# Set numbers of spare matmuls before the first batch's waits, and new due times throughout

## The chip, the core and the metric

The kernel runs on one core of a Trainium2 chip. The metric is device time in microseconds for one launch: the median of three runs before the change is 1341.77 us (1341.25 to 1344.07). Lower is better. TensorE is called PE in profiles, its weight loads PEld, VectorE is DVE, ScalarE is ACT, GpSimd is POOL, and SP is the engine whose queue issues nearly all DMA transfers.

## The reference

Attention over 32 learned memory slots (8 batches, 8 heads, 576 tokens, 64 wide), then two feed-forward layers over the 4608 tokens (512 to 2048 to 512, twice). Cut to what is computed:

```
a = softmax(phi over tokens);  k_m = a.T @ k;  v_m = a.T @ v
attn = softmax(q @ k_m.T / 8) @ v_m            # per batch and head
h = x @ w_in;   r = max(h, 0);  x = (s * r * r + b) @ w_out
h = x @ w1;     out = (h * sigmoid(1.702 * h)) @ w2
```

The weights are float64 in HBM and are turned into float32 on the chip.

## The kernel before, in words

The program is a list of operations, each with a due time, the engines that could run it with a cost on each, and the tiles it reads and writes. `Order.sort` (lines 90 to 184) is a list scheduler: it keeps a clock for each engine and always takes the ready operation that can start first, with rank (due time less a correction in the table `EARLIER`) deciding between several. What it writes out is one fixed order of instructions on each engine. Its clocks are only its own reckoning; on the chip each engine goes through its instructions in that order and waits at semaphores.

There are three large stages: eight batches of attention with the first matrix product; the product with `w_out` (the function `down`); and the second layer (`up`, then `last`). All large products run as three float32r matmuls (high and low halves of each operand), and the two large stages use a seven-product scheme for blocks, so that most of the DVE's and ACT's time goes to additions and to splitting operands.

The change is strongest in the opening of the first batch, where PE has no large product to do yet. Its chain on PE, by the names of the PSUM tiles:

- `warm`: ten matmuls of the identity with itself, of no use to the result.
- `s` (`slots`, line 586): two transposes of the maxima `am`; two that spread the negated maxima `nm`; 32 small products of `ph` (the exponentials) with `kv`, in two groups of 16, one per half of the heads (`mm`, line 631); eight more for the last 64 tokens (`last`, line 637); two transposes of the scaled result `an`. ACT then copies the slot keys `km`.
- `x` (`beside`, line 692): scores of `q` with `km`, in two pieces of 384 and 192 columns; each is copied to `sc` and folded back by transposes into `a` (line 727).
- `vw` (`matrix`, line 826): the slot values times the converted `w_in` block; ACT rounds it to `mh`, and PE subtracts `mh` from `vw` in place (line 850), which ACT copies to `ml`.
- `y` (line 740): transposes of the weights `st` after the softmax, from which ACT and DVE make `ah` and `al`.
- `h` (`step`, line 856): the first large product. From here on PE has dense work to the end.

When an operation on PE opens a PSUM tile, `pst` (line 274) may put spare matmuls ahead of it: each multiplies the 128 x 128 float32 identity by itself into the tile that is about to be overwritten. `Order.sort` sets their number just before the operation (line 163): the gap that the scheduler's own clock has there, in us, times `FILL` = 2.5. Tiles `x` and `a` of the first batch get none (line 276), and the second group of 16 and the last eight of `s` get none, since they open no tile. Spare matmuls go on until tile `warm` is opened a second time at the third block of the first batch (line 1484).

Of the kernel before, what the change touches and what calls it, by code (L numbers as in the profile page):

```python
# [18 lines left out]
P = 128  # L19
# [8 lines left out]
class Order:  # L28
# [4 lines left out]

    FILL, AHEAD, SLACK = 2.5, 120, 0.3

    EARLIER = {
        ('t', ('u4', 'wo', 5), 0): 16,
        ('t', ('e', 'w1', 0, 2)): -5,  # L40
        ('w', ('wi', 1, 0), 1): -3,
        ('w', ('mh', 0, 0)): -15,
        ('t', ('st', 0, 0)): -3,
        ('t', ('ol', 'wo', 2, 1, 1)): 5,
        ('t', ('al', 0, 0), 1): 1,
        ('t', ('ol', 'wo', 5, 1, 'A')): 14,
        ('sm', ('a', 1, 0, (0, 1))): 1,
        ('t', ('ah', 1, 0), 0): -3,
        ('w', ('w1', 7, 0, 1), 'l'): -12,
        ('sm', ('a2', 0, 1)): 21,  # L50
        ('t', ('sw1', 0, 0)): -12,
        ('t', ('A', 'wo', 0, 1)): -2,
        ('w', ('raw', ('w', ('wi', 1, 1)), 1), 0): 2,
        ('w', ('raw', ('w', ('wi', 1, 0)), 0), 0): -2,
        ('t', ('C', 'wo', 5, 3)): 5,
    }

    NEAR = 4
# [5 lines left out]
    def __init__(self, bufs):  # L64
        self.bufs, self.ops, self.rank, self.fill, self.until, self.since = bufs, [], [], None, 0, 0
        self.narrow = set()
        self.slot = {}
        self.wrote, self.read, self.users = {}, {}, {}

    def add(self, due, ways, r=(), w=(), first=0):  # L70

        n = len(self.ops)
        deps, new = set(), []
        for k in r:
            deps |= self.wrote[k]
            self.read.setdefault(k, set()).add(n)
        for k in w:
            deps |= self.wrote.get(k, set()) | self.read.get(k, set())
            self.wrote[k], self.read[k] = {n}, set()
        for x in dict.fromkeys(k[:2] for k in (*r, *w) if k[0] in self.bufs):  # L80
            if x not in self.users:
                self.users[x] = []
                new.append(x)
            self.users[x].append(n)
        deps.discard(n)
        due = max([due] + [self.ops[d][0] for d in deps])
        self.ops.append((due, ways, deps, new))
        self.rank.append(due - first - self.EARLIER.get(w[0] if w else None, 0))

    def sort(self):  # L90
# [22 lines left out]
        while ready:  # L113
            can = {}
            limit = ready[0][0] + self.AHEAD
            for due, n in ready:
                if due > limit and can:
                    break
                _, ways, deps, new = ops[n]
                t0 = 0.0  # L120
                if new:
                    ok = True
                    for tag in {x[0] for x in new}:
                        mine = [x for x in new if x[0] == tag]
                        f = free[tag]
                        if len(f) < len(mine) or any(x not in queue[tag][:len(f)] for x in mine):
                            ok = False
                            break
                        t0 = max(t0, f[0][0] if len(mine) == 1 else heapq.nsmallest(len(mine), f)[-1][0])
                    if not ok:  # L130
                        continue
                best = None
                for i, (eng, cost, _, port) in enumerate(ways):
                    t = max(t0, at.get(eng, 0.0))
                    if port:
                        t = max(t, held["dve" if eng == "pool" else "pool"])
                    for d in deps:
                        e = end[d] + (self.LAG[eng] if on[d] != eng else 0.05)
                        if e > t:
                            t = e  # L140
                    score = t + cost * self.WEIGHT.get(eng, 1.0)
                    if best is None or score < best[0]:
                        best = score, t, eng, i
                can.setdefault(best[2], []).append((best[1], due, n, best[3]))
            if not can:
                raise RuntimeError("no order")
            first = []
            for tag, v in can.items():
                t0 = min(v)[0]
                like = [c for c in v if c[0] <= t0 + 0.1 and c[2] in self.narrow and c[1] >= self.since] if tag == "pe" and run else ()  # L150
                if like:
                    c = min(like, key=lambda c: c[1:])
                    if c[1] < min(v, key=lambda c: c[1:])[1] + self.NEAR:
                        first.append(c)
                        continue
                first.append(min((c for c in v if c[0] <= t0 + (self.SLACK if c[1] < self.until else 0.0)), key=lambda c: c[1:]))
            t, _, n, i = min(first)
            _, ways, _, new = ops[n]
            eng, cost, fn, port = ways[i]
            if port:  # L160
                held[eng] = t + cost
            if self.fill and eng == "pe":
                out.append(lambda n=int((t - at.get(eng, 0.0)) * self.FILL): self.fill and self.fill(n))
            for x in new:
                queue[x[0]].remove(x)
                self.slot[x] = heapq.heappop(free[x[0]])[1]
            at[eng], on[n] = t + cost, eng
            end[n] = t + cost + self.END_LAG.get(eng, 0.0)
            ready.remove((rank[n], n))
            if eng == "pe":  # L170
                run = n in self.narrow
            out.append(fn)
            for m in after[n]:
                left[m] -= 1
                if not left[m]:
                    bisect.insort(ready, (rank[m], m))
            for x in of[n]:
                last[x] = max(last[x], end[n])
                uses[x] -= 1
                if not uses[x]:  # L180
                    heapq.heappush(free[x[0]], (last[x] + 0.2, self.slot[x]))
# [5 lines left out]
class Net:  # L187
# [27 lines left out]
    COL = 0.463  # L215

    FIRST = 100
    HEAD1 = (-51.0, 2.9, 16.5)
    PARTS1 = (-0.8, -1.7, -3.5)
    SCORES1 = (-34.0, 6.0, 7.5)  # L220
    COUPLES1 = (7.8, -36, 6.5)
    LEADS1 = (20, 17, 11, 10.0, 3, 1.6, 11.0, 1.3)
    VALUES1 = (-31.0, -1.6, 7.6, 28.4)
    VALUES = (-6.5, -9.4, 0.0, -1.9)
    NEXT1, NEXT = (6.0, 6.5), (-0.4, 1.9)
    ROWS1, ROWS = (24.5, 1.7, 0.3), (11, 10.5, 2.0)
    POOL1 = ((0, 1), (0,), (0,), (0,))
    TURN1 = (1, 1, 1, 1)
    EITHER1 = 0
    WAIT = 0  # L230
    OUT1 = (-12.1, 11.5)

    B1, B2 = 40, 58.5

    TS, N = 384, 6
    PAS, AT = 2.0892857142857144, 5
    PREP = (30, 100, 148.5, 222)

    def __init__(self, nc, tc, ctx, aps):
        self.nc, self.tc, self.a = nc, tc, aps  # L240
# [32 lines left out]

    def pst(self, k):
        x = self.t(k, [P, 2, 512])
        for _ in range(min(self.spare, 0) if k[1][0] in ('x', 'a') and k[1][1] == 0 else self.spare):
            self.nc.tensor.matmul(x[:, 0, 0:P], self.ident, self.ident, start=True, stop=True)
        self.spare = 0
        return x

    def dram(self, name, *index, cols=768):

# [303 lines left out]
    def slots(self, b, due, apart, lead=8):  # L586
# [25 lines left out]
        d = ds[1]  # L612
# [3 lines left out]
        for g in range(2):  # L616
# [13 lines left out]

            def mm(g=g, ph=ph, fs=fs):
                out = T[z] if g else self.pst(z)
                for c in range(4):
                    for h in range(4):
                        nc.tensor.matmul(out[32 * h:32 * h + 32, g, 0:129], T[ph][:, h, :, c], T[fs[h]][:, c], start=(c == 0), stop=False)
# [4 lines left out]
                        r = slice(64 * g, 64 * g + 64)  # L640
                        nc.tensor.matmul(T[z][32 * h:32 * h + 32, g, 0:129], T[phs[g]][r, h, :, 4], T[f1][r, h], start=False, stop=True)

            self.pe(d + 4, 2070, mm, (ph, *fs), (z,), narrow=True)
        self.pe(d + 4.5, 880, last, (*phs, f1), (z,), narrow=True)
        an = [("t", ("an", b, g)) for g in range(2)]

# [268 lines left out]
        us = range(t // self.HS, -(-(t + self.TS) // self.HS))  # L915
        self.dma(due, lambda: self.two(k).rearrange("p a b -> p (a b)"), lambda: self.rows(i, j, t, self.TS), [("r", i, j, u) for u in us], (k,), 384)

    FIRST2 = {1: -2.75, 6: -1.5, 7: 0.0, 5: 1.75, 3: 6.75, 'Y': 6.25, 4: 4.0}
    ODD2 = {1: -3.5, 6: 0.5, 7: 1, 5: 2, 'A': 4, 'B': 5, 3: 4, 4: 5.5, 'D': 6.5}
    EVEN2 = {1: -3.25, 6: 0, 7: 1, 5: 2, 3: 4, 'Y': 5, 4: 5.5}  # L920
    END2 = {1: -4, 6: 0, 7: 1, 5: 2, 'A': 3.25, 'B': 5, 3: 3, 4: 5, 'D': 5}
    ADDS = (0, 1, 2, 3, 4)
    LONG2 = {'Y': 1, 'A': 0.75, 'B': 0.75, 'D': 0.5}
    W1 = (30, 105, 2)
    LEAD2, EARLY2, AHEAD2, OD2, CC2 = 15, 9, 15.5, 1, 9

    def down(self, s, due):

# [330 lines left out]
            for k, t in ((old, s - 1), (new, s)):  # L1259
                self.out(due + 2, t, q, k)  # L1260

    HEAD = {1: -2.5, 6: 0, 7: 1, 5: 2, 'Y2': 2.5, 3: 3.5, 4: 5.5}
    MID = {1: -3, 6: -0.25, 7: 1.25, 5: 2.25, 'Y': 4.25, 'A': 4.75, 4: 5.25, 'B': 6.25, 'D': 7.25}
    END = {1: -3, 6: 0, 7: 1.25, 5: 2.25, 'A2': 3.25, 3: 3.75, 'B2': 4.75, 4: 5.75, 'D2': 5.75}
    AHEAD, OD, CC, RAW = 6, 3.0, 4.5, 2
    LONG = {'Y': 0.25, 'A': 0.75, 'B': 0.25, 'D': 0.25}
    EARLY, LEAD, BEGIN, T4 = 10.5, 8, -7.0, -6.8

    def last(self, s, due):

# [370 lines left out]
```

## Time and profile before

| | |
|---|---|
| median of three runs | 1341.77 us |
| the profiled execution | 1343.54 us, its span 1341.8 us |
| PE busy | 1326.7 us (99%) |
| DVE busy | 1147.3 us (86%) |
| ACT busy | 877.1 us (65%) |
| mean granted TensorE clock | 0.996 of 2.4 GHz |
| DMA moved | 381.29 MB, 284 GB/s |

PE is busy nearly all the time, so the interesting figure is its idle time, 15 us in all, and where it lies. A row of the time line that says `x20` holds 20 merged instructions; the number behind the start is the time from the first one's start to the last one's end, and in square brackets stands the idle time before the row and what ended it. Since matmuls overlap, the distance between the starts of two rows says what a row cost PE.

### The profile page before, as it was taken

How to read it: one execution, taken by the hardware profiler on the slowest of the kernel's cores; microseconds unless marked ns; L12 is line 12 of the kernel's file. 1: busy time of each engine (PE TensorE's matmuls, PEld its weight loads, DVE VectorE, ACT ScalarE, POOL GpSimd, SP SyncE). 2: the span in 40 equal slices, each digit the busy share in tenths (PEclk: the TensorE clock that was granted, in tenths of full speed). 3: DMA queues.
4: the chain of work that ended last, by engine and by line, in shares of the span. 5: the costliest groups of instructions: out<-in, count | busy, mean ns of one | idle time of the engine just before them, and what ended most of it. 6: DMA issues, size and time to landing. Idle time of an engine off the chain costs nothing.

```text
span 1341.8 us, 24315 instructions
## 1 busy us (share of the span) xinstructions
PE 1326.7 (99%) x9042; PEld 1284.1 (96%) x9042; DVE 1147.3 (86%) x1712; ACT 877.1 (65%) x1233; POOL 117.2 (9%) x112
## 2 busy tenths in 40 slices
PE   7999999999999999999999999999999999999998
PEld 5888888899999999999999999999999999999998
DVE  6887898999999999999997989696477698988985
ACT  4766666697877787889775666565464365655644
POOL 2201231100001000100100000000000011101011
PEclk8999999999999999999999999999999999999999
DMA  9988999896877695798799699879599978878984
GB/s 367 356 303 313 349 330 358 290 370 218 304 261 185 176 347 153 225 340 295 205 353 354 251 371 358 329 264 348 191 372 386 310 217 250 205 231 234 296 210 92
DMA packets 155959, 381.29 MB, mean 284 GB/s; under 512 B 17344, under 2 KB 30528, under 8 KB 155840
## 3 DMA queue, kind: packets, MB, share of 16 engines
q1 hardware_dynamic: 146048, 362.23, 75.7%
q0 software_dynamic: 9792, 17.50, 8.8%
q8 instruction: 71, 1.16, 0.3%
q14 instruction: 48, 0.39, 0.1%
HBM read 226.12 MB, written 153.55 MB: 283 GB/s over the span
## 4 chain that ended last, share of the span: by engine, by line
PE 94%; DVE 2%; DMA 2%; ACT 1%; issue 0%; SPq 0%; POOL 0%; POOLq 0%; ACTq 0%; DVEq 0%
PE h L344 5%; PE X L974 5%; PE X L975 5%; PE X L1182 5%; PE X L976 5%; PE X L1181 5%; PE X L1180 5%; PE h L346 5%; PE h L345 5%; PE X L1318 4%; PE X L1317 4%; PE X L1316 4%; PE Y L1182 2%; PE Y L1181 2%; PE Y L1180 2%; PE Y L975 2%
## 5 line engine op out<-in xcount | busy, mean ns | idle before, releaser
L344 PE MATMUL h<-ah,mh 128*128 128x288 f32 x512 | 156.0, 305 | 0.0
L320 DVE TENSOR_TENSOR ol<-A,oh 128x768 fp32r<-128x768 f32 x144 | 136.1, 954 | 22.5 <-ACT oh L314 12.6
L346 PE MATMUL h<-ah,ml 128*128 128x288 f32 x512 | 151.0, 295 | 0.1
L345 PE MATMUL h<-al,mh 128*128 128x288 f32 x512 | 150.7, 294 | 0.0
L314 ACT CAST oh<-A 128x768 fp32r<-128x768 f32 x125 | 107.3, 868 | 39.4 <-DVE A L320 18.9
L872 ACT ACTIVATE r<-h 128x576 f32<-128x576 f32 x127 | 89.5, 706 | 64.1 <-PE h L346 57.5
L974 PE MATMUL X<-oh,wo 128*128 128x384 f32 x384 | 128.5, 335 | 0.0
L975 PE MATMUL X<-ol,wo 128*128 128x384 f32 x384 | 128.4, 334 | 0.0
L976 PE MATMUL X<-oh,wo 128*128 128x384 f32 x384 | 128.3, 334 | 0.0
L1180 PE MATMUL X<-oh,w 128*128 128x384 f32 x384 | 128.3, 334 | 0.0
L1181 PE MATMUL X<-ol,w 128*128 128x384 f32 x384 | 128.3, 334 | 0.0
L1182 PE MATMUL X<-oh,w 128*128 128x384 f32 x384 | 128.3, 334 | 0.0
L344 PEld LDWEIGHTS h<-ah,mh 128*128 128x128 f32 x512 | 96.3, 188 | 17.4 <-issue 9.6
L1316 PE MATMUL X<-oh,w 128*128 128x384 f32 x320 | 107.0, 334 | 0.0
L1318 PE MATMUL X<-oh,w 128*128 128x384 f32 x320 | 106.9, 334 | 0.0
L346 PEld LDWEIGHTS h<-ah,ml 128*128 128x128 f32 x512 | 96.1, 188 | 0.3 <-ACT ml L853 0.3
L320 DVE TENSOR_TENSOR ol<-B,oh 128x768 fp32r<-128x768 f32 x96 | 89.8, 953 | 7.5 <-PE X L1318 3.6
L1317 PE MATMUL X<-ol,w 128*128 128x384 f32 x288 | 96.2, 334 | 0.0
L345 PEld LDWEIGHTS h<-al,mh 128*128 128x128 f32 x512 | 96.2, 188 | 0.0
L314 ACT CAST oh<-B 128x768 fp32r<-128x768 f32 x89 | 76.3, 870 | 25.9 <-DVE B L320 13.2
L974 PEld LDWEIGHTS X<-oh,wo 128*128 128x128 f32 x384 | 72.1, 188 | 0.4 <-ACT u L1000 0.4
L975 PEld LDWEIGHTS X<-ol,wo 128*128 128x128 f32 x384 | 72.1, 188 | 0.2 <-DVE ol L320 0.2
(323 smaller groups left out, 3818.0 us busy)
## 6 DMA issues: line engine op xcount, KB each, us to landing
w<-w SPq DMA_DIRECT2D x84, 512.0 KB, 5.9
r<-r SPq DMA_DIRECT2D x128, 288.0 KB, 4.7
kv<-in_kv SPq DMA_DIRECT2D x72, 258.0 KB, 5.4
g<-u SPq DMA_DIRECT2D x48, 384.0 KB, 4.2
raw<-in_w SPq DMA_DIRECT2D x32, 512.0 KB, 5.8
q<-in_q SPq DMA_DIRECT2D x32, 288.0 KB, 5.6
A<-r SPq DMA_DIRECT2D x24, 384.0 KB, 5.5
B<-r SPq DMA_DIRECT2D x24, 384.0 KB, 5.7
```

Source lines behind the costliest of these rows:

```text
L314: self.order.add(due, [self.act(n, lambda: nc.scalar.copy(out(), src()), psum), self.dve(n, lambda: nc.vector.tensor_copy(out(), src()), f ...
L320: self.order.add(due, [self.dve(n, lambda: nc.vector.tensor_tensor(out(), a(), b(), op=op), port=port)], r, w, first)
L344: self.nc.tensor.matmul(ps, wh, xh, start=start and i == 0, stop=False)
L345: self.nc.tensor.matmul(ps, wh, xl, start=False, stop=False)
L346: self.nc.tensor.matmul(ps, wl, xh, start=False, stop=(i == n - 1))
L974: nc.tensor.matmul(out, T[w][:, 0, c], T[h][:, p], start=f, stop=False, skip_group_check=True)
L975: nc.tensor.matmul(out, T[w][:, 0, c], T[l][:, p], start=False, stop=False, skip_group_check=True)
L976: nc.tensor.matmul(out, T[w][:, 1, c], T[h][:, p], start=False, stop=last, skip_group_check=True)
L1180: nc.tensor.matmul(out, T[w][:, 0, c], T[h][:, k], start=f, stop=False, skip_group_check=True)
L1181: nc.tensor.matmul(out, T[w][:, 0, c], T[l][:, k], start=False, stop=False, skip_group_check=True)
L1182: nc.tensor.matmul(out, T[w][:, 1, c], T[h][:, k], start=False, stop=k == 1, skip_group_check=True)
L1316: nc.tensor.matmul(out, T[w][:, 0, c], T[h][:, p], start=f, stop=False, skip_group_check=True)
```

## The change

The number of spare matmuls no longer follows from the scheduler's gaps but from a table, `SPARE`, keyed by the tiles that the operation writes. The second group of `s` and the scores `x` may have them too. Nearly all tables of due times have new values, and `EARLIER` has 27 entries in place of 17.

```diff
+    SPARE = {
+        (('ps', ('s', 0, 0)),): 12,
+        (('ps', ('s', 0, 2)),): 15,
+        (('ps', ('s', 0, 2)), ('ps', ('s', 0, 2), 1)): 29,
+        (('ps', ('s', 0, 3)),): 10,
+        (('ps', ('x', 0, 0)),): 13,
+        (('ps', ('vw', 0, 0)),): 8,
+        (('ps', ('y', 0, 0)),): 26,
+        (('ps', ('h', 0, 0, 0)),): 19,
+        (('ps', ('y', 0, 1)),): 4,
+        (('ps', ('h', 0, 0, 1)),): 7,
+        (('ps', ('s', 1, 0)),): 5,
+    }
...
-        ('t', ('e', 'w1', 0, 2)): -5,
+        ('t', ('e', 'w1', 0, 2)): -6,
...
+        self.opens.append(tuple(w))
...
-                out.append(lambda n=int((t - at.get(eng, 0.0)) * self.FILL): self.fill and self.fill(n))
+                out.append(lambda n=self.SPARE.get(self.opens[n], 0): self.fill and self.fill(n))
...
-    HEAD1 = (-51.0, 2.9, 16.5)
+    HEAD1 = (-53.0, 0.4, 32.0)
...
-    EITHER1 = 0
+    EITHER1 = 1
...
     def pst(self, k):
         x = self.t(k, [P, 2, 512])
-        for _ in range(min(self.spare, 0) if k[1][0] in ('x', 'a') and k[1][1] == 0 else self.spare):
-            self.nc.tensor.matmul(x[:, 0, 0:P], self.ident, self.ident, start=True, stop=True)
+        self.idle(x, 0)
+        return x
+
+    def idle(self, x, g):
+        for _ in range(self.spare):
+            self.nc.tensor.matmul(x[:, g, 0:P], self.ident, self.ident, start=True, stop=True)
         self.spare = 0
-        return x
...
             def mm(g=g, ph=ph, fs=fs):
                 out = T[z] if g else self.pst(z)
+                if g:
+                    self.idle(out, 1)
...
-            self.pe(d + 4, 2070, mm, (ph, *fs), (z,), narrow=True)
+            self.pe(d + 4, 2070, mm, (ph, *fs), (z, (*z, 1)) if g else (z,), narrow=True)
...
-    ODD2 = {1: -3.5, 6: 0.5, 7: 1, 5: 2, 'A': 4, 'B': 5, 3: 4, 4: 5.5, 'D': 6.5}
+    ODD2 = {1: -3.5, 6: 0.5, 7: 1, 5: 1.5, 'A': 4, 'B': 5, 3: 4, 4: 5.5, 'D': 7.0}
...
-    EARLY, LEAD, BEGIN, T4 = 10.5, 8, -7.0, -6.8
+    EARLY, LEAD, BEGIN, T4 = 8.0, 7, 11.5, -4.8
```

On PE, from the spread of `nm` to the transposes of `an` in the first batch, before (`L277 ... ident` are the spare matmuls, `kv_160` holds the last 64 tokens; the numbers only tell tiles apart):

```order
L277 MATMUL s_136<-ident 128x128
L609 MATMUL s_136<-ident,nm_131 128x128 x2
L277 MATMUL s_162<-ident 128x128 x11
L635 MATMUL s_162<-kv_140,ph_96 32x129
...
L635 MATMUL s_162<-kv_110,ph_98 32x129
L641 MATMUL s_162<-kv_160,ph_96 32x129
...
L277 MATMUL s_245<-ident 128x128 x3
L609 MATMUL s_245<-ident,an_238 128x128
```

The same place on PE in the changed kernel (the spare matmuls are `L307` there, `kv_151` holds the last 64 tokens):

```order
L638 MATMUL s_140<-ident,nm_133 128x128 x2
L307 MATMUL s_153<-ident 128x128 x15
L666 MATMUL s_153<-kv_104,ph_85 32x129
...
L307 MATMUL s_153<-ident 128x128 x29
L666 MATMUL s_153<-kv_185,ph_98 32x129
...
L672 MATMUL s_153<-kv_151,ph_98 32x129
L307 MATMUL s_274<-ident 128x128 x10
L638 MATMUL s_274<-ident,an_268 128x128
L638 MATMUL s_274<-ident,an_270 128x128
L307 MATMUL x_296<-ident 128x128 x13
```

The spare matmuls ahead of the first group go from 11 to 15, 29 new ones stand between the two groups, those ahead of `an` go from 3 to 10, and 13 new ones stand ahead of the scores `x`.

On PE from the first fold `a` to the first large product `h`, before:

```order
L727 MATMUL a_284<-ident,sc_266 128x128 x3
L840 MATMUL vw_294<-wi_133,km_251 32x512 x2
...
L727 MATMUL a_308<-ident,sc_266 128x128 x2
L850 MATMUL vw_294<-mh_334,less 128x512 x2
L740 MATMUL y_350<-ident,st_314 128x128 x6
L277 MATMUL h_381<-ident 128x128 x6
L344 MATMUL h_381<-ah_361,mh_334 128x288
```

The same stretch of PE in the changed kernel:

```order
L758 MATMUL a_335<-ident,sc_324 128x128 x3
L307 MATMUL vw_353<-ident 128x128 x8
L871 MATMUL vw_353<-wi_138,km_290 32x512 x2
...
L758 MATMUL a_376<-ident,sc_324 128x128 x2
L307 MATMUL y_404<-ident 128x128 x26
L771 MATMUL y_404<-ident,st_373 128x128 x6
L881 MATMUL vw_353<-mh_396,less 128x512 x2
L307 MATMUL h_468<-ident 128x128 x19
L373 MATMUL h_468<-ah_445,mh_396 128x288
```

There are now 8 spare matmuls ahead of `vw`, 26 ahead of `y`, and 19 in place of 6 ahead of `h`; `y` stands ahead of the subtraction of `mh`.

On ACT around the copy of the scores to `sc`, before (`raw` and `wi` belong to the conversion of `w_in`):

```order
L314 COPY km_251<-s_245 128x256
L749 COPY sc_268<-x_257 128x384
L430 ACTIVATE raw_219<-raw_219 128x512
L749 COPY sc_268<-x_270 128x192
L423 ACTIVATE wi_303<-raw_232 128x512
```

The same place on ACT in the changed kernel:

```order
L343 COPY km_290<-s_274 128x256
L780 COPY sc_320<-x_296 128x384
L780 COPY sc_324<-x_296 128x384
L780 COPY sc_324<-x_326 128x192
L459 ACTIVATE raw_249<-raw_249 128x512
```

Both halves of the first piece are now copied by ACT, one behind the other; before, DVE copied one of them.

In the whole program the opening has 158 spare matmuls, `warm`'s ten among them, where it had 48: 10, 12, 15, 29, 10, 13, 8, 26, 19, 4, 7 and 5, in the order of the program, in place of 10, 10, 1, 11, 3, 6, 2, 3 and 2. The first nine of the new numbers stand ahead of the first `h`, the last three (4, 7, 5) behind it; of the old ones the first six stand ahead of it and 2, 3, 2 behind it.

## Rows read from the trace of the kernel before

**Rows 1.** Busy time by engine in stretches: bounds, length, PE, PEld, DVE, ACT, POOL, clock, DMA.

```profile
0.00:34.50 34.50, 25.15 (x234) 20.72 (x235) 23.12 (x39) 16.87 (x29) 8.59 (x11) 0.85 0.97 368
60.00:1300.00 1240.00, 1238.57 (x8340) 1204.92 (x8339) 1075.50 (x1598) 824.52 (x1151) 96.02 (x91) 1.00 0.86 287
1300.00:1342.00 42.00, 37.65 (x214) 36.69 (x212) 24.51 (x37) 16.48 (x24) 4.39 (x5) 1.00 0.43 99
380.00:730.00 350.00, 349.44 (x2011) 348.02 (x2010) 337.17 (x495) 276.97 (x384) 22.80 (x25) 1.00 0.81 260
```

**Rows 2.** Time line of PE in the opening: start, length, instructions, [idle before <-releaser].

```profile
1.37 4.64 PE L277 MATMUL warm<-ident 128*128 128x128 f32 x20 [1.37 <-POOL ident masks.py:199]
5.80 3.14 PE L277 MATMUL s<-ident 128*128 128x128 f32 x20
...
9.95 2.62 PE L277 MATMUL s<-ident 128*128 128x128 f32 x22
12.50 2.30 PE L635 MATMUL s<-kv,ph 128*32 128x129 f32 x64
16.84 0.49 PE L641 MATMUL s<-kv,ph 64*32 64x129 f32 x16 [2.04 <-DMA kv<-in_kv]
17.26 1.37 PE L277 MATMUL s<-ident 128*128 128x128 f32 x6
19.28 0.73 PE L609 MATMUL s<-ident,an 128*128 128x128 f32 x2 [0.65 <-ACT an L657]
20.47 2.35 PE L722 MATMUL x<-q,km 64*32 64x384 f32 x32 [0.46 <-ACT km L314]
...
24.65 1.09 PE L840 MATMUL vw<-wi,km 64*32 64x512 f32 x16
25.67 0.66 PE L727 MATMUL a<-ident,sc 128*128 128x128 f32 x4
30.20 0.73 PE L850 MATMUL vw<-mh,less 128*128 128x512 f32 x2 [3.87 <-ACT mh L314]
31.00 1.30 PE L740 MATMUL y<-ident,st 128*128 128x128 f32 x6
32.10 2.73 PE L277 MATMUL h<-ident 128*128 128x128 f32 x12
34.52 0.45 PE L344 MATMUL h<-ah,mh 128*128 128x288 f32 x1
...
36.25 0.60 PE L277 MATMUL y<-ident 128*128 128x128 f32 x4
36.69 0.60 PE L740 MATMUL y<-ident,st 128*128 128x128 f32 x4
```

**Rows 3.** Clock and busy time in three stretches of the opening, columns as in Rows 1.

```profile
17.50:24.50 7.00, 5.36 (x46) 3.50 (x45) 4.02 (x9) 2.68 (x7) 3.02 (x3) 0.51 1.03 404
24.50:31.20 6.70, 2.76 (x26) 1.12 (x25) 6.30 (x10) 6.31 (x12) 1.07 (x1) 1.00 1.03 410
31.20:34.60 3.40, 3.40 (x19) 3.40 (x17) 2.92 (x6) 3.23 (x7) 0.82 (x1) 0.51 1.02 405
```

**Rows 4.** Time line of ACT and DVE in the opening, columns as in Rows 2.

```profile
22.23 1.00 DVE L751 COPY sc<-x 128x384 f32<-128x384 f32 x2 [1.55 <-PE x L722]
22.82 0.48 ACT L749 COPY sc<-x 128x384 f32<-128x384 f32 x1 [2.40 <-DVE sc L751]
...
29.91 0.94 DVE L760 TENSOR_TENSOR st<-st,a 128x768 f32<-128x768 f32 x1
33.23 1.02 DVE L320 TENSOR_TENSOR al<-y,ah 128x384 fp32r<-128x384 f32 x2 [0.45 <-ACT ah L314]
```

**Rows 5.** Transfers issued before 30 us: line, count, size, median us from issue to landing.

```profile
q<-in_q SPq DMA_DIRECT2D x4, 288.0 KB, 7.2
```

**Rows 6.** SP's issue of the transfers of q: start, length, count.

```profile
10.84 2.38 SPq L304 DMA_DIRECT2D q<-in_q  x4
```

**Rows 7.** PE's waits over the whole span: total us, times, longest.

```profile
PE Z L1088 <- ACT zw L1098: 0.6, 1, 0.6
```

More of the change, by code (lines that the diff above doesn't have):

```diff
@@ L28 @@
 class Order:
+    SPARE = {
[11 more added lines that the diff above has]
+    }
     FILL, AHEAD, SLACK = 2.5, 120, 0.3
     EARLIER = {
-        ('t', ('u4', 'wo', 5), 0): 16,
-        ('t', ('e', 'w1', 0, 2)): -5,
+        ('t', ('e', 'w1', 0, 2)): -6,
         ('w', ('wi', 1, 0), 1): -3,
[L42 to L50, printed above, removed]
-        ('t', ('sw1', 0, 0)): -12,
[L52 to L55, printed above, removed]
+        ('w', ('mh', 0, 0)): -7,
+        ('t', ('ol', 'wo', 2, 1, 1)): 19,
+        ('t', ('al', 0, 0), 1): 3,
+        ('t', ('sw1', 0, 0)): -12,
+        ('w', ('raw', ('w', ('wi', 2, 1)), 0), 0): 3,
+        ('sm', ('a2', 0, 1)): 15,
+        ('t', ('C', 'wo', 5, 0)): -8,
+        ('t', ('q', 0, 3)): 1,
+        ('w', ('wi', 0, 1), 1): 13,
+        ('t', ('q', 0, 1)): 13,
+        ('w', ('raw', ('w', ('wi', 1, 1)), 1), 0): 3,
+        ('t', ('sc', 0, 1), 1): 5,
+        ('t', ('D', 'wo', 4, 2)): 3,
+        ('t', ('ol', 'x', 1, 'A')): -8,
+        ('t', ('kv', 0, 8)): 1,
+        ('t', ('sc', 0, 0), 0): 15,
+        ('t', ('u2', 'wo', 3), 1): 5,
+        ('t', ('kv', 0, 1)): 11,
+        ('t', ('al', 0, 0), 0): 18,
+        ('nm', (0, 'r')): 16,
+        ('w', ('wi', 0, 1), 0): 6,
+        ('t', ('kv', 0, 0)): 9,
+        ('w', ('raw', ('w', ('wi', 0, 0)), 0), 0): 21,
+        ('w', ('ph', 0, 0)): 8,
+        ('t', ('q', 0, 2)): 8,
     }
@@ L67, in __init__ @@
         self.slot = {}
+        self.opens = []
         self.wrote, self.read, self.users = {}, {}, {}
@@ L217 @@
     FIRST = 100
-    HEAD1 = (-51.0, 2.9, 16.5)
[L219 to L228, printed above, removed]
-    EITHER1 = 0
+    HEAD1 = (-53.0, 0.4, 32.0)
+    PARTS1 = (0.0, -2.2, 0.4)
+    SCORES1 = (-34.0, 5.0, 8.0)
+    COUPLES1 = (7.8, -37.5, 6.0)
+    LEADS1 = (19.5, 19, 11, 12.0, 3, 1.8, 10.0, 2.7)
+    VALUES1 = (-30.0, -0.1, 15.1, 29.4)
+    VALUES = (-8.5, -5.4, 1.2, -0.9)
+    NEXT1, NEXT = (6.0, 4.0), (-1.9, 2.1)
+    ROWS1, ROWS = (25.5, 1.2, -2.7), (12.5, 5.5, -11.3)
+    POOL1 = ((0,), (0,), (0,), (0, 1))
+    TURN1 = (1, 1, 0, 1)
+    EITHER1 = 1
     WAIT = 0
-    OUT1 = (-12.1, 11.5)
+    OUT1 = (-11.1, 11.5)
     B1, B2 = 40, 58.5
@@ L236 @@
     PAS, AT = 2.0892857142857144, 5
-    PREP = (30, 100, 148.5, 222)
+    PREP = (29.5, 97, 144.5, 220.5)
     def __init__(self, nc, tc, ctx, aps):
@@ L916, in load @@
         self.dma(due, lambda: self.two(k).rearrange("p a b -> p (a b)"), lambda: self.rows(i, j, t, self.TS), [("r", i, j, u) for u in us], (k,), 384)
-    FIRST2 = {1: -2.75, 6: -1.5, 7: 0.0, 5: 1.75, 3: 6.75, 'Y': 6.25, 4: 4.0}
-    ODD2 = {1: -3.5, 6: 0.5, 7: 1, 5: 2, 'A': 4, 'B': 5, 3: 4, 4: 5.5, 'D': 6.5}
-    EVEN2 = {1: -3.25, 6: 0, 7: 1, 5: 2, 3: 4, 'Y': 5, 4: 5.5}
-    END2 = {1: -4, 6: 0, 7: 1, 5: 2, 'A': 3.25, 'B': 5, 3: 3, 4: 5, 'D': 5}
+    FIRST2 = {1: -3.0, 6: -1.5, 7: 0.5, 5: 1.5, 3: 5.75, 'Y': 6.25, 4: 5.25}
+    ODD2 = {1: -3.5, 6: 0.5, 7: 1, 5: 1.5, 'A': 4, 'B': 5, 3: 4, 4: 5.5, 'D': 7.0}
+    EVEN2 = {1: -3.25, 6: -0.25, 7: 1, 5: 2, 3: 4, 'Y': 5, 4: 5.5}
+    END2 = {1: -4, 6: 0, 7: 1, 5: 2, 'A': 3.25, 'B': 5.25, 3: 3, 4: 5, 'D': 5.5}
     ADDS = (0, 1, 2, 3, 4)
-    LONG2 = {'Y': 1, 'A': 0.75, 'B': 0.75, 'D': 0.5}
+    LONG2 = {'Y': 1, 'A': 0.75, 'B': 0.75, 'D': 0.25}
     W1 = (30, 105, 2)
-    LEAD2, EARLY2, AHEAD2, OD2, CC2 = 15, 9, 15.5, 1, 9
+    LEAD2, EARLY2, AHEAD2, OD2, CC2 = 15, 12.0, 12.5, 1, 10.5
     def down(self, s, due):
@@ L1260, in phase @@
                 self.out(due + 2, t, q, k)
-    HEAD = {1: -2.5, 6: 0, 7: 1, 5: 2, 'Y2': 2.5, 3: 3.5, 4: 5.5}
+    HEAD = {1: 0.25, 6: 1.0, 7: 0.75, 5: 2.25, 'Y2': 5.0, 3: 4.25, 4: 5.75}
     MID = {1: -3, 6: -0.25, 7: 1.25, 5: 2.25, 'Y': 4.25, 'A': 4.75, 4: 5.25, 'B': 6.25, 'D': 7.25}
-    END = {1: -3, 6: 0, 7: 1.25, 5: 2.25, 'A2': 3.25, 3: 3.75, 'B2': 4.75, 4: 5.75, 'D2': 5.75}
-    AHEAD, OD, CC, RAW = 6, 3.0, 4.5, 2
-    LONG = {'Y': 0.25, 'A': 0.75, 'B': 0.25, 'D': 0.25}
-    EARLY, LEAD, BEGIN, T4 = 10.5, 8, -7.0, -6.8
+    END = {1: -3, 6: 0.75, 7: 2.25, 5: 2.25, 'A2': 3.25, 3: 3.75, 'B2': 5.0, 4: 6.0, 'D2': 5.75}
+    AHEAD, OD, CC, RAW = 6, 2.5, 12.0, 1
+    LONG = {'Y': 0.5, 'A': 1.25, 'B': 0.5, 'D': 0.25}
+    EARLY, LEAD, BEGIN, T4 = 8.0, 7, 11.5, -4.8
     def last(self, s, due):
```

## The prediction

> **What bounds the kernel now.** I read the stretches of busy time first, since PE is at 99%. From 60 to 1300 us PE is busy 1238.57 of 1240 us, in the last 42 us all but 4.35, and in the first 34.5 us only 25.15 [rows 1]. So of PE's 15 idle us 9.35 lie ahead of the first large product `h`, and 1.4 in the long middle. Whatever the change does to the order of the middle, PE has no more than that to win there; what it does ahead of `h` moves everything behind it one for one, because nothing later has slack to take it up. Next comes the time line of PE in the opening [rows 2]. The reader is to see two kinds of loss there: waits (2.04 us for the last `kv`, 3.87 for `mh`, two of about half a microsecond) and pieces that run at the lower of the clock's two levels. The stretches of 17.5 to 24.5 and 31.2 to 34.6 us show a granted clock of 0.51, that is 1.2 GHz, the one between them 1.00 [rows 3]. PE had waited shortly before each of the two. Both losses are what spare matmuls can act on, and both are paid with PE time when a spare matmul outlasts its wait.
>
> **The price of one spare matmul.** The order before holds ten in `warm`; the time line has 20 rows for them [rows 2]: each float32 spare is two instructions on PE. At full clock, 22 instructions (11 spares) reach from 9.95 to 12.50, 0.116 us each with the change of tile behind them; four (2 spares) from 36.25 to 36.69, 0.110 each. I take 0.112, so 0.224 us for a spare, with 0.220 and 0.232 as ends. At half clock `warm` takes 4.43 us for ten, 0.443 each [rows 2].
>
> The Trainium skill (TensorE: Matmul & The Clock Gate, Back-to-back issue gap) gives about 81 ns as the sustained distance between matmuls of 128 columns, 56 ns for an isolated pair. By that 29 spares would take 2.3 us, an estimate from that page, where the row's price makes 6.5. The trace does not agree for these float32 matmuls, and the sum goes by the row.
>
> **The walk to `h`.** The order of PE is fixed, and spares wait for nothing but PE itself, so I go along the changed order with the distances of the time line, at full clock after about 7 us, as in the trace (the spares behind `warm` take 20 instructions in 2.98 us, between the two prices) [rows 2, 3].
> - `warm` is unchanged. 12 spares in place of 10 ahead of `am`: +0.45, so the spares that stood at 9.95 start at 10.40. The one spare ahead of `nm` that goes lay in the wait for `nm` and is worth nothing.
> - 15 in place of 11: +0.90. The first group of 16 starts at 13.85, where it stood at 12.50.
> - From 12.50 to 17.26 the two groups and the eight of the last tokens took 4.76 us, 2.04 of it the wait for `kv`, 2.72 work. That wait goes: `kv` had landed at 16.8, is now issued earlier, and PE comes later. In its place stand 29 spares, 6.50 us. The next spares start at 13.85 + 2.72 + 6.50 = 23.07.
> - 10 spares, 2.24: 25.3. The transposes of `an` came 1.95 us after the last product had ended (17.33 to 19.28), so `an` is ready at 25.1, and the spares cover it.
> - Transposes of `an`, 0.22 at full clock; 13 spares, 2.91: `x` starts at 28.4. `km` is there 1.2 us after the transposes (19.28 to 20.47), at 26.5. The last `q` was issued by 13.2 and lands 7.2 us later, at 20.4 [rows 5, 6]. Both are early.
> - `x` took from 20.47 to 22.23, until its first copy began [rows 4], at half clock, so about 0.9 at full. Both copies now run on ACT, 0.48 each [rows 4], 0.96, a lag of 0.1, and the second half of the fold, 0.33: 30.7.
> - 8 spares, 1.79: `vw` at 32.5. `vw` to the second fold 1.02 (24.65 to 25.67), four transposes 0.44: 33.95.
> - 26 spares, 5.82: `y` at 39.8. The softmax behind `a` ended at 30.85 [rows 4], 6.2 after the fold (24.65); now 30.7 + 6.2 = 36.9, so it is covered, by 2.9.
> - `y` 0.66; the subtraction 0.45. Its `mh` came 5.55 after the start of `vw` (24.65 to 30.20), so at 38.05, before PE is there. 40.9.
> - 19 spares, 4.26: `h` starts at 45.2. `ml`, `ah` and `al` ended 2.15 us after `y` did (32.10 to 33.23 + 1.02) [rows 2, 4], at 42.7: covered, by 2.5.
>
> `h` stood at 34.52, so this is +10.7. Behind it, 4, 7 and 5 spares in place of 2, 3 and 2, with PE dense and its operands now long there: 9 x 0.224 = +2.0. Together +12.7, less some 0.2 for small waits in the first batch that an earlier conversion of `w_in` hides: **+12.5**.
>
> A second way checks it. 110 spares more cost 24.6 us. Against that go the idle time ahead of `h`, 9.35 less the first 1.37 and about 0.8 that stay, 7.2; and half of the 5.36 and 3.40 busy us at half clock [rows 3], 4.4. That is +13.0. With the two prices of a spare the sum ranges over 0.9 us; with the whole of it 11.5 to 13.5.
>
> **The later stages.** New due times reorder `down`, `up` and `last`. PE's products are the same in number and size. The cover is deep: 1.4 us of waits in 1240. DVE is the next engine, 337.17 of 350 us in `down` [rows 1], so an order that makes it late shows at once; the longest single wait of that kind costs 0.6 [rows 7]. No row shows the new order's waits. Bounds: -1.4 (all those waits go) and +4 (about six more like the longest). I take 0, as the number of products and additions is the same. The tail's 4.35 us are the last copies and stores, which stay.
>
> **Sum.** The profiled execution took 1343.54 us, 1341.8 of it the span; with 12.5 it takes 1356.0. It ran 1.8 above the median of the three runs, so the median goes from 1341.77 to **1354.3**, 0.93% slower.
>
> **Rivals.**
> 1. *The spares fit the waits, and the clock stays up: faster.* Place: from 10.40 to the landing of `q` at 20.4 there are 10.0 us, 2.9 of work, and 67 spares: they fit if one costs at most 0.106 us. Ahead of `y` there are 6.2 less 1.5 for 34 spares, 0.138 each; ahead of `h` 2.15 for 19, 0.113. So below about 0.11 us a spare, one instruction rather than two, `x` starts at 20.6 at full clock, `y` at 29.1 in place of 31.00, and `h` about 3 us earlier: 1339. For it: waits and half clock are in the trace just where the table puts its numbers. Against it: 20 rows for ten spares, and 0.112 for each row. The 81 ns of the Trainium skill (TensorE: Matmul & The Clock Gate, Back-to-back issue gap) would bring this case about. Chance 0.04.
> 2. *Given back later.* PE starts late, all other engines do not, so `w_in` and operands are ready sooner. But PE can only get back what it idles: 1.4 us in the middle: 1352.9. Chance 0.10, since some of it is likely.
> 3. *New waits in the middle.* The new places in `down` or `last` make DVE late at the +4 bound: 1358. For it: 96% of DVE in `down`. Against: the same additions, and the first batch leaves it more lead. Chance 0.10.
> 4. *The table finds no operation* (a key that doesn't match), so fewer spares than told. The changed order has all 158 of them, so this can only hold in part: about the time of before, 1341.8. Chance 0.03.
>
> My own forecast has 0.73. Since rivals 2 and 3 are slower too, slower by over 0.2% (2.7 us, about what this kernel's runs can tell apart) has 0.93, no change 0.03, faster 0.04. The range takes in the price's ends and rivals 2 and 3, with a microsecond for another chip at either end: 1350 to 1359.
>
> **What would show it.** In the changed kernel's time line 58 rows of spares between the two groups of `s`, about 6.5 us long, with no wait for `kv` behind them; PE idle ahead of `h` near 1 us beside the first 1.37; clock 1.00 from 8 us on; `h` at 45 us, give or take one; PE's busy time up by some 20 us; 60 us to the end unchanged in idle time. It is wrong if spares stand with one row each, if `h` starts before 40 us, or if the middle shows waits over 5 us in sum.

## The result

The changed kernel takes 1353.1 us (median of four runs, 1350.86 to 1354.47) where the kernel before takes 1342.0: a ratio of 1.0079, 95% interval 1.0059 to 1.0098. It is slower by 11.1 us. The forecast was 1354.3 and slower, with 1350 to 1359 as its range.

The profiled execution took 1354.47 us, 10.9 more than that of before, and its span 1352.7. Busy time by engine in three stretches of the changed kernel, columns as in [rows 1]:

```profile
0.00:44.50 44.50, 42.30 (x434) 39.35 (x435) 22.73 (x42) 19.26 (x34) 4.95 (x9) 1.00 0.91 347
60.00:1300.00 1240.00, 1237.36 (x8417) 1201.67 (x8416) 1079.48 (x1602) 818.50 (x1146) 98.16 (x93) 1.00 0.86 288
1311.00:1353.00 42.00, 38.32 (x222) 38.00 (x220) 25.71 (x39) 17.03 (x24) 4.39 (x5) 1.00 0.43 98
```

PE idles 2.20 us ahead of `h` where it idled 9.35 [rows 1], the clock is 1.00, and yet `h` is late. The middle idles 2.6 us where it idled 1.4, the last 42 us 3.7 where they idled 4.35. The time line of PE in the opening of the changed kernel, columns as in [rows 2]:

```profile
1.36 4.63 PE L307 MATMUL warm<-ident 128*128 128x128 f32 x20 [1.36 <-POOL ident masks.py:199]
5.79 2.90 PE L307 MATMUL s<-ident 128*128 128x128 f32 x24
...
9.70 3.51 PE L307 MATMUL s<-ident 128*128 128x128 f32 x30
13.14 1.12 PE L666 MATMUL s<-kv,ph 128*32 128x129 f32 x32
14.19 6.74 PE L307 MATMUL s<-ident 128*128 128x128 f32 x58
20.86 1.12 PE L666 MATMUL s<-kv,ph 128*32 128x129 f32 x32
21.92 0.48 PE L672 MATMUL s<-kv,ph 64*32 64x129 f32 x16
22.33 2.50 PE L307 MATMUL s<-ident 128*128 128x128 f32 x20
24.66 0.38 PE L638 MATMUL s<-ident,an 128*128 128x128 f32 x2
24.88 3.07 PE L307 MATMUL x<-ident 128*128 128x128 f32 x26
27.88 1.20 PE L753 MATMUL x<-q,km 64*32 64x384 f32 x32
29.39 0.93 PE L758 MATMUL a<-ident,sc 128*128 128x128 f32 x6 [0.32 <-ACT sc L780]
30.16 1.95 PE L307 MATMUL vw<-ident 128*128 128x128 f32 x16
32.04 1.09 PE L871 MATMUL vw<-wi,km 64*32 64x512 f32 x16
...
33.55 5.97 PE L307 MATMUL y<-ident 128*128 128x128 f32 x52
39.36 0.82 PE L771 MATMUL y<-ident,st 128*128 128x128 f32 x6
39.94 0.71 PE L881 MATMUL vw<-mh,less 128*128 128x512 f32 x2
40.48 4.40 PE L307 MATMUL h<-ident 128*128 128x128 f32 x38
44.64 0.38 PE L373 MATMUL h<-ah,mh 128*128 128x288 f32 x1
```

The reader is to see that the waits of [rows 2] for `kv` and `mh` are gone (no brackets), that each spare is still two rows (29 of them are `x58`), and that the place of the waits is taken by spares that last longer: 6.67 us (14.19 to 20.86) where PE had waited 2.04, 5.81 ahead of `y`, 4.16 ahead of `h`. The last `kv` was issued at 8.82 us here and landed 6.1 us later, at 14.9, so behind the first group (14.19) some 0.7 us were left to wait, and 29 spares stand there. `h` starts at 44.64, +10.1 against [rows 2].

### The profile page after: what moved, and what is told of

The parts are those of the page before. It is cut to its first block, busy times and chain, and to the rows that moved or that the text cites. A ratio compares the mean times of both kernels' runs of the same rounds, so it can differ in the third digit from the quotient of the medians.

```text
span 1352.7 us, 24676 instructions
## 1 busy us (share of the span) xinstructions
PE 1344.5 (99%) x9260; PEld 1304.3 (96%) x9260; DVE 1151.1 (85%) x1715; ACT 871.4 (64%) x1230; POOL 114.8 (8%) x112
## 4 chain that ended last, share of the span: by engine, by line
PE 97%; DMA 2%; ACT 1%; DVE 0%; issue 0%; POOL 0%; POOLq 0%; ACTq 0%; DVEq 0%
PE h L373 5%; PE h L375 5%; PE h L374 5%; PE X L1213 5%; PE X L1212 5%; PE X L1211 5%; PE X L1005 5%; PE X L1007 5%; PE X L1006 5%; PE X L1347 4%; PE X L1348 4%; PE X L1349 4%; PE Y L1007 2%; PE Y L1213 2%; PE Y L1212 2%; PE Y L1006 2%
## 5 line engine op out<-in xcount | busy, mean ns | idle before, releaser
L349 DVE TENSOR_TENSOR u<-Y,u 128x768 f32<-128x768 f32 (+1 forms) x50 | 46.8, 937 | 34.8 <-ACT u L1223 22.3
```

Of the source, the lines that this page charges most:

```text
L349: self.order.add(due, [self.dve(n, lambda: nc.vector.tensor_tensor(out(), a(), b(), op=op), port=port)], r, w, first)
```

## The experiments

The theory: a spare holds PE for 0.224 us at the upper clock whether the data have come or not, so a table about twice as large as the waits makes PE the bound of the opening. The rivals: the new order costs, and the spares lie in waits; or it is their number or place, through PSUM tiles or the queue, and not their PE time.

**Half the numbers.** All of `SPARE` halved, the rest as changed.

```diff
-        (('ps', ('s', 0, 2)), ('ps', ('s', 0, 2), 1)): 29,
+        (('ps', ('s', 0, 2)), ('ps', ('s', 0, 2), 1)): 14,
...
-        (('ps', ('y', 0, 0)),): 26,
+        (('ps', ('y', 0, 0)),): 13,
```

> The changed kernel with every number of SPARE halved (81 spares with warm's ten, in place of 158); order and due times as changed. Theory (a spare holds PE 0.224 us, so the table's numbers are about twice what the waits hold): the spares now fit the waits, h starts at 31.5 to 33 us in place of 44.6, the clock stays at its upper level or nearly, and the time is 1339 to 1341 us, below both kernels. Rival (the new order costs, the spares lie in waits): h stays near 44 and the time near 1353. Rival (halfway: spares cost in proportion, no wait to fill): about half of the loss stays, 1347.

Measured: 1338.93 us (1337.46 to 1342.71), 0.9978 of before, 0.9969 to 0.9988. So it is below both kernels. The profiled execution is the one of 1342.71 us. PE's time line there:

```profile
12.12 3.39 PE L307 MATMUL s<-ident 128*128 128x128 f32 x28
17.48 1.12 PE L666 MATMUL s<-kv,ph 128*32 128x129 f32 x32 [1.96 <-DMA kv<-in_kv]
...
28.18 3.07 PE L307 MATMUL y<-ident 128*128 128x128 f32 x26
31.62 0.87 PE L771 MATMUL y<-ident,st 128*128 128x128 f32 x6 [0.38 <-DVE st L791]
...
34.73 0.38 PE L373 MATMUL h<-ah,mh 128*128 128x288 f32 x1
```

Waits stand behind the spares again: those are short enough now. `h` at 34.73 misses the expected 31.5 to 33 in this execution. PE could go on only at 17.48, when `kv` had landed, where the last run below shows 15.34, and behind that wait the clock is at 0.51 from 18.7 to 22.2 us. The median of the runs lies at the lower end of the theory's 1339 to 1341.

**The new order with the old rule for spares.**

```diff
-                out.append(lambda n=self.SPARE.get(self.opens[n], 0): self.fill and self.fill(n))
+                out.append(lambda n=int((t - at.get(eng, 0.0)) * self.FILL): self.fill and self.fill(n))
...
-                if g:
-                    self.idle(out, 1)
...
-        self.idle(x, 0)
+        if k[1][0] in ('x', 'a') and k[1][1] == 0:
+            self.spare = 0
+        self.idle(x, 0)
```

> The changed kernel's order and due times with the old rule for spares (gap of the scheduler's clock times 2.5, none for x and for the second group of s): 55 spares. Theory: the order by itself costs nothing; h at 33 to 35 us, 1340 to 1343 us, the same as before within what can be measured. Rival (the new order costs): 1350 or more.

Measured: 1340.71 us, 0.9991 of before, 0.9982 to 1.0000, as expected; `h` stands at 31.69 us, earlier than the 33 to 35 expected. The new order and due times cost nothing that these runs can tell; this rival falls.

**The old order with the table.** The kernel before with `SPARE`, `opens` and `idle` of the change.

```diff
+    SPARE = {
+        (('ps', ('s', 0, 0)),): 12,
...
+                if g:
+                    self.idle(out, 1)
```

> The order and due times of before, with the table SPARE and the two new places for spares: 158 spares. Theory: the spares alone make the loss; PE dense from 1.4 us to h, which starts at 44 to 45 us, 1351 to 1354 us. Rival (the new order costs): 1342 to 1344.

Measured: 1358.41 us, 1.0124 of before, 1.0108 to 1.0139. The table alone makes the loss, but more of it than expected, by some 5 us: `h` starts at 50.00. PE's time line in this kernel, and then its clock in two stretches (columns as in [rows 1]):

```profile
5.80 3.70 PE L296 MATMUL s<-ident 128*128 128x128 f32 x24
...
30.79 0.88 PE L747 MATMUL a<-ident,sc 128*128 128x128 f32 x6 [0.91 <-ACT sc L769]
...
37.18 0.74 PE L870 MATMUL vw<-mh,less 128*128 128x512 f32 x2 [2.11 <-ACT mh L332]
37.75 7.59 PE L296 MATMUL y<-ident 128*128 128x128 f32 x52
45.18 0.82 PE L760 MATMUL y<-ident,st 128*128 128x128 f32 x6
...
50.00 0.38 PE L362 MATMUL h<-ah,mh 128*128 128x288 f32 x1
```

```profile
34.40:38.30 3.90, 1.79 (x19) 1.45 (x12) 3.83 (x7) 3.90 (x8) 1.22 (x1) 1.00 1.04 392
38.30:41.70 3.40, 3.40 (x18) 3.40 (x17) 1.40 (x3) 0.85 (x1) 0.67 (x1) 0.50 0.88 310
```

In the old order the subtraction of `mh` stands ahead of `y`'s spares, so PE waits 2.11 us for `mh` with nothing to do, and behind that wait the clock is at 1.2 GHz for 3.4 us, in which `y`'s 52 rows go on: 7.43 us (37.75 to 45.18) for 5.81 in the changed kernel. These two make 3.7 of the 5.4 us; 0.6 is a longer wait for `sc` (0.91 for 0.32), and 0.8 is that the first 24 rows of spares behind `warm` take 3.70 us for 2.90, so the clock rose later at the start. So the change of order is worth some microseconds to a kernel with this table, by putting spares into the wait for `mh`, and 1.4 by the medians without it, as the run before this showed, which its interval can hardly tell from nothing.

**No spares but `warm`'s ten.**

```diff
+    SPARE = {}
```

> The changed order with warm's ten spares alone. Theory: PE waits as the data come, 14 us or so of idle time ahead of h, with the clock at its lower level for much of it, so that products on the chain take twice their time: h at 33 to 35 us and the first large products at half clock for some us, 1342 to 1346 us, 7 or more below the changed kernel. If the clock is worth more than the spares cost: 1353 or more.

Measured: 1340.95 us, 0.9992 of before, 0.9982 to 1.0001; `h` at 32.08. Two waits of PE and three stretches of the clock in it:

```profile
16.35 1.95 PE L654 MATMUL s<-kv,ph 128*32 128x129 f32 x32 [2.88 <-DMA kv<-in_kv]
...
30.39 1.04 PE L759 MATMUL y<-ident,st 128*128 128x128 f32 x6 [3.16 <-DVE st L779]
```

```profile
10.40:24.10 13.70, 8.37 (x118) 4.96 (x115) 7.83 (x15) 5.21 (x12) 1.62 (x1) 0.50 1.04 401
24.10:30.90 6.80, 3.58 (x29) 1.46 (x28) 6.42 (x11) 6.60 (x12) 1.36 (x1) 1.00 1.03 411
30.90:37.70 6.80, 6.52 (x23) 4.74 (x21) 6.15 (x12) 6.00 (x11) 1.29 (x1) 0.50 1.03 401
```

Some 20 us at the lower clock, and yet it is 12 us below the changed kernel, and below the 1342 to 1346 that the theory gave. The slow pieces ahead of the waits for `kv` and for the softmax on DVE (`st`) cost nothing, since those 2.88 and 3.16 us take them up: `h` starts at 32.08, and at 31.95 in the run with fitted numbers below. The third stretch lies on the first large products, and it does cost. The first product of `down`, here and then in that run:

```profile
294.27 0.34 PE L993 MATMUL X<-oh,wo 128*128 128x384 f32 x1
292.39 0.34 PE L1005 MATMUL X<-oh,wo 128*128 128x384 f32 x1
```

So from `h` to `down` PE takes 262.19 us here and 260.44 there. These 1.75 us are about what the medians of the two best tables (half and fitted) lie below this one's, 2.0 and 1.7; the intervals against before meet. So what spares win over none in this opening is no more than about 2 us, and by these two profiles it is the clock behind `h`.

**Cheaper spares in the same numbers and places.** A float32r tile in place of the float32 identity, behind `warm`.

```diff
+        w = self.less if self.warmed else self.ident
         for _ in range(self.spare):
-            self.nc.tensor.matmul(x[:, g, 0:P], self.ident, self.ident, start=True, stop=True)
+            self.nc.tensor.matmul(x[:, g, 0:P], w, w, start=True, stop=True)
```

> The changed kernel with the table as it is, but every spare behind warm's ten multiplies the float32r tile `less` by itself in place of the float32 identity: one instruction on PE, not two. Theory (only the PE time of a spare counts, not how many there are or where): a 288-column float32r product stands 0.133 us from the next, so a 128-column one costs 0.06 to 0.09; 148 of them cost 9 to 13 us, which the waits hold; h at 32 to 35 us and 1338 to 1342 us. Rival (the places of the spares or their number cost, through PSUM tiles or the queue): 1350 or more.

Measured: 1340.68 us (1338.95 to 1346.91), 0.9987 of before, 0.9977 to 0.9998. All 158 spares are there, and the loss is gone, so number and place cost nothing that these runs can tell: this rival falls too. The profiled execution is the one of 1346.91 us. PE's time line there, its weight loads for the spares between the groups, and its clock behind the wait for `kv` (columns as in [rows 1]):

```profile
12.10 3.45 PE L309 MATMUL s<-less 128*128 128x128 f32 x29
17.51 1.12 PE L668 MATMUL s<-kv,ph 128*32 128x129 f32 x32 [1.96 <-DMA kv<-in_kv]
...
21.68 3.02 PE L309 MATMUL x<-less 128*128 128x128 f32 x13
...
37.37 0.35 PE L375 MATMUL h<-ah,mh 128*128 128x288 f32 x1
```

```profile
12.09 3.31 PEld L309 LDWEIGHTS s<-less 128*128 128x128 f32 x29 [0.18 <-issue]
```

```profile
18.60:28.80 10.20, 10.20 (x86) 8.20 (x84) 5.40 (x11) 5.30 (x13) 1.35 (x1) 0.50 1.03 410
```

29 spares are 29 rows now. Less the 0.28 us that one of them lasts by itself, their 3.45 us are 28 distances of 0.113. That is half, as the number of instructions says, and not the 0.06 to 0.09 that I had expected from the wide products. `h` at 37.37 lies outside the expected 32 to 35: behind the wait for `kv` the clock is at 0.50 for 10.2 us, and there the 13 spares ahead of `x` take 0.226 each. So this execution wins back 7.3 of the 10.1 us of `h`; that all of the loss is gone is read from the median of ten.

**More spares where PE has no wait.** 52 ahead of `y` in place of 26.

```diff
-        (('ps', ('y', 0, 0)),): 26,
+        (('ps', ('y', 0, 0)),): 52,
```

> The changed kernel with 52 spares ahead of y in place of 26. Theory: PE has no wait left there, so each of the 26 more costs its full 0.224 us: +5.8, h at 50.4 us and 1359 us, 1.0043 times the changed kernel. Rival (spares cost less than their rows say, since part lies in a wait): +3 or less, 1356 or below.

Measured: 1357.35 us (1356.82 to 1359.48), 1.0115 of before, 1.0102 to 1.0129, so 4.3 us above the changed kernel by the medians, between the two expectations. The profile is plainer:

```profile
33.78 11.78 PE L307 MATMUL y<-ident 128*128 128x128 f32 x104
45.39 0.82 PE L771 MATMUL y<-ident,st 128*128 128x128 f32 x6
...
50.67 0.38 PE L373 MATMUL h<-ah,mh 128*128 128x288 f32 x1
```

104 rows take 11.61 us, 5.80 more than 52 did: 0.223 a spare. `h` is 6.0 later, and so is the first product of `down` (310.93 us for 304.90), so up to there the full price is paid. Less of it arrives at the end: 4.3 us by the medians, and 2.5 between the two profiled executions (spans of 1355.2 and 1352.7). From that product of `down` to the end this one takes 3.5 us less. It waits less there: between 300 and 1300 us PE idles 0.86 us in it and 2.63 in the changed kernel's. A wait costs more than the idle time shown, since products overlap: in the changed kernel one that shows 0.47 us of idle time (ahead of 638.37 us) has the next product start 0.81 us behind the one before, where 0.17 is usual. Those few waits differ from one profile to the next, and a difference of a microsecond or two between medians can't be read off `h` alone.

**Numbers fitted to the waits.**

```diff
-        (('ps', ('s', 0, 0)),): 12,
+        (('ps', ('s', 0, 0)),): 3,
...
-        (('ps', ('h', 0, 0, 0)),): 19,
+        (('ps', ('h', 0, 0, 0)),): 7,
```

> The changed order with numbers fitted to the waits that the runs with half the spares and with none showed: 3, 7, 12, 5, 2, 3, 10, 7, 3, 0, 0 in the table's order (62 with warm's ten). Theory: h at 31 to 33 us with the clock up, 1337.5 to 1340 us, at or a little below the run with half the spares (1338.9). If the number of spares hardly matters once they fit: 1338.5 to 1341, the same as half, as the old rule and as none.

Measured: 1339.3 us (1337.29 to 1342.08, 11 runs), 0.9980 of before, 0.9971 to 0.9989. PE's time line:

```profile
15.34 1.12 PE L666 MATMUL s<-kv,ph 128*32 128x129 f32 x32 [0.84 <-DMA kv<-in_kv]
...
29.29 0.88 PE L771 MATMUL y<-ident,st 128*128 128x128 f32 x6 [0.79 <-DVE st L791]
...
31.95 0.38 PE L373 MATMUL h<-ah,mh 128*128 128x288 f32 x1
```

`h` stands at 31.95, with waits under 1 us left. It is as fast as half the table and beats both kernels by an interval that lies below 1; between it and half there is no difference to be told; 1339.3 lies in the ranges of both expectations.

## Why the prediction was right

- *The price.* 0.224 us for a spare, from two rows at 0.112. The longest row of spares, 104 instructions in 11.61 us, gives 0.223. The rule of the Trainium skill (TensorE: Matmul & The Clock Gate, Back-to-back issue gap), 81 ns for 128 columns, does not hold for these operands: 0.112 for one float32 instruction of two, 0.113 for a float32r product. The range that the prediction gives the sum for the two ends of the price, 0.9 us, is too small: 0.012 us on 110 spares are 1.3; the bounds of the forecast took in more than that.
- *The walk.* `x` was forecast at 28.4 and came at 27.88, `y` at 39.8 (39.36), `h` at 45.2 (44.64). The difference is there from the start: the spares behind `warm` took 24 rows in 2.74 us (5.79 to 8.53), where before 20 took 2.98, so the clock rose earlier in this execution; the same 24 rows took 2.96 in the kernel with 52 spares ahead of `y`. So this part of the miss is chance, and not a wrong step of the walk. From `am` on, 0.7 early, the walk holds within 0.3 us. All waits that it called covered were covered.
- *Behind `h`.* +2.0 was forecast for nine more spares. They ran, but the first product of `down` starts at 304.90 us where it started at 294.45: 10.45 later, only 0.3 more than the first `h` was. So 1.7 of this term was given back within the batches, 0.2 of it forecast: the term was over-sized. Two parts of it can be read. PE idles 0.01 us in this stretch where it idled 0.30. And the changed kernel's `TURN1` (1, 1, 0, 1 for 1, 1, 1, 1) takes the subtraction of `mh` off PE for one block of the first batch, six products where there were eight (before, then changed: count, shortest, median and longest in ns, first and last start in us):

```profile
L850 PE MATMUL vw<-mh,less x8: 387/397/496, 30.2 to 66.1; 128*128 128x512 f32 x8
L881 PE MATMUL vw<-mh,less x6: 387/396/477, 39.9 to 76.8; 128*128 128x512 f32 x6
```

  Such a pair took 0.56 us before (43.97 to 44.53), and the prediction did not count it. Where the other 0.8 lies no run separates, the smaller products of the batches standing in another order too.
- *The later stages.* Taken at 0, with -1.4 and +4 as bounds: +1.2 of idle time in the middle, two waits of 0.8 and 0.9 us among it, as the changed kernel's waits of PE show (total, times, longest):

```profile
PE Z L1460 <- ACT z L1478: 0.9, 1, 0.9
PE Z L1461 <- DVE ol L349: 0.8, 1, 0.8
```

- *The tail.* Taken as unchanged; it idles 0.7 us less, 3.68 of the last 42 where it was 4.35 [rows 1], which offsets about half of that.
- *Sum.* +12.5 forecast, +11.1 measured by the medians, +10.9 by the profiles: 0.6 less in the walk (10.1 for 10.7), 1.5 less behind `h` (0.3 for 1.8), and 0.5 more in the later stages and the tail together.
- *The rivals.* The second (given back later) and the third (new waits in the middle) each came true in a small part, 1.5 us behind `h` and 1.2 in the middle. The first (the spares fit) was priced at 1339 us and bounded at 0.106 to 0.138 us a spare. Spares of half the number (1338.9) and of half the price (1340.7) both go to that side. It was a good price for a case that the table misses by a factor of two. That half of the table's spares, or fewer, fill the waits is shown (the kernels with 62 and 81 spares are the two best); why the table has these numbers is not a question that a run can settle.

## What to carry to other kernels

A spare matmul is work that PE does in its place in the order. It doesn't end when the data come, so count the instructions that the trace shows for it (two for float32 here), take their distance, and give each wait less than it holds; too few cost little (none at all was 12 us better than twice too many). Ahead of a dense stretch to the end, PE time too much arrives in the total for the greater part: the 10.1 us of `h` were 10.9 in the profiles, the 6.0 of the longer row ahead of `y` 4.3 in the medians. Before filling a wait to keep the clock up, look at what ends it: where it is a landing or another engine's chain, a faster piece of PE ahead of it wins nothing, and one behind it wins only its own length. In the kernel without spares the stretch at 1.2 GHz that cost time was the one on the first large products.

## What was not expected of the hardware

The float32r products of 128 columns stand 0.113 us apart in the run with cheaper spares. The first ones of 288 columns stand 0.132 apart, ten steps from 34.80 to 36.12 in the kernel before:

```profile
34.80 0.30 PE L345 MATMUL h<-al,mh 128*128 128x288 f32 x1
...
36.12 0.29 PE L346 MATMUL h<-ah,ml 128*128 128x288 f32 x1
```

So the price does not go with the number of columns. The narrow products' weight loads, 29 in 3.31 us at 0.19 each, stand 0.111 apart, as the products do; whether the loads set the price no run separates.

And landings at the start vary between executions, with the same order of transfers. The last `kv` of the second group ended PE's wait at 17.5 us in the profile with half the spares and at 15.3 us in that with fitted numbers. Of these 2.1 us 0.6 are a later issue (9.70 us for 9.12), and 1.5 are the transfer itself, 7.6 us from issue to landing for 6.1. The runs of the kernel with half the spares lie between 1337.5 and 1342.7 us.
